# Half-size products from tile 4 on, tile 1 masked by VectorE, three general heads, a stepped write and engine orders from a table

## The chip, the cores and the metric

The kernel runs on one core of a Trainium2 chip. A core has five engines that run side by side and meet through semaphores: TensorE (PE, matrix products; PEld is its weight load), VectorE (DVE), ScalarE (ACT), GpSimd (POOL) and SyncE (SP, which here issues DMA). Matrix products go to an accumulator memory of eight banks per partition, which the program calls `banks`; ACT and DVE read them from there. The metric is the device time of one execution in microseconds (us).

## The reference

Causal attention with 4 batches, 8 heads, 768 positions and head size 64, and behind it a two-layer network over 3072 tokens:

```python
scores = scale * np.matmul(q, k.transpose(0, 1, 3, 2))
...
stream_keep = causal & (is_sink | in_win)
...
mask = np.where(retr[0, :, 0, 0, None, None], full_mask, stream_mask)
...
a = a / (np.sum(a, axis=-1, keepdims=True) + 1e-09)
return np.matmul(a, v).astype(np.float32)
```

```python
h = x @ w_in
g = h - np.tanh(h)
return (g @ w_out).astype(np.float32)
```

Retrieval heads (`is_retrieval`, three of eight here: heads 0, 2 and 6) see all earlier positions. The five other heads see only the first 4 positions (sinks) and a window of the last 64. `w_in` is 512 x 2048, `w_out` 2048 x 512.

## The kernel before

The 3072 tokens are cut into 12 tiles of 256 (`TT`), three per batch (`NG`); a tile is two blocks of 128. Heads go in pairs, `hp` 0 to 3, one head of a pair in partitions 0 to 63 and the other in 64 to 127.

**Attention of a tile.** q, k and v are loaded and turned to 16 bit. Up to tile 2, TensorE transposes q and k (`st_T`); from tile 3 on (`FROM`) a DMA does (`turn`). `st_S` (L1265) makes the scores of a pair, in groups of up to 512 columns per head, and ACT takes the exponential (L1362). `st_A` (L1421) multiplies with V; a column of ones gives the sum, DVE inverts it (L1462) and scales (L1474, L1489). Tiles 0 and 1 get their mask from TensorE, which adds it to the scores ahead of the products (`add`; `MASKS` is 2). Tile 0 uses per-head diagonals (`by_head`, L1308 and L1311), tile 1 the table `m4` (`masks`, L1074 and L1084, used in L1327). From tile 2 on DVE multiplies the exponentials with a mask (`mask`, L1371).

**Ranks.** `by_rank` (L1092) computes on the chip which heads are retrieval heads and sorts them to the front. From tile 3 on, GpSimd gathers q, k and v by rank (`gather`, L805). The first four ranks (`NGEN`) are general: they compute all earlier blocks, with a mask by flag. The last four are near heads: a query block takes its own block and the one before, and the sinks are packed into copies (`kc`, `vf`, by `gather` and `spread`). A pair is either general or near (`is_near`). A second program at the end repeats everything without ranks if more than `NGEN` heads are retrieval heads.

**The two layers.** `H_unit` (L1549) makes 2 x 128 columns of the first layer for 256 tokens, ACT the tanh (L1578) and DVE the difference (L1585) into `gt`. The second layer exists in two forms. `O_group` (L1614) has 16 products of 512 columns per block of 128 tokens, and ACT scales them out (L1598). From tile `ST` = 7 on, a scheme for 2 x 2 blocks takes seven products in place of eight: each has half the depth and half the columns, 8 matmuls of 256 columns (`piece`, L1725). For it DVE adds and subtracts parts of `gt` in fp16 (`sums`, L1700) and, once, parts of `w_out` (`combine`, L1660). The products come together again by ACT (`take`, L1783), DVE (`fold`, L1802) and POOL (`add`, L1813); `STEPS` says in which of the eight units of the next tile. In every third such tile (`mixed`), the tokens of a pair of rows are dealt out to the two halves, so the first layer reads x with a step of two.

**Order.** The program is not written in engine order. Each operation is given to `Plan` (L145) with an engine, an estimated duration and what it reads and writes. `Plan.run` simulates the engines when the kernel is built, picks on each the waiting operation with the lowest priority number, and emits the instructions in that order. The number is the place in the program plus an entry of the table `NUDGE`. Constants such as `CUT`, `LEAD`, `LD`, `GA` and `TWHEN` say beside which unit the attention, the loads, the gathers and the combinations are put. Each engine then runs its instructions strictly in the emitted order. DMAs are issued from SP, POOL and ACT.

Of the kernel before, what the change touches and what calls it, by code (L numbers as in the profile page):

```python
# [12 lines left out]
TT = 256  # L13
# [3 lines left out]
NUDGE = {  # L17
# [127 lines left out]
class Plan:  # L145
# [11 lines left out]
    GRAB = 350  # L157
    RESULT = {"PE": 200, "ACT": 0, "DVE": 0, "POOL": 0, "SP": 0}

    def __init__(self, bufs, nudge):  # L160
        self.bufs, self.nudge = bufs, nudge
        self.users = {}
        self.ops = []
# [223 lines left out]
def kernel(  # L387
# [109 lines left out]
    ST = 7  # L497
# [1755 lines left out]
```

## Time and profile before

| what | value |
|---|---|
| median of 3 runs | 226.71 us (226.59 to 226.87) |
| the profiled execution | 228.01 us |
| its span, first to last instruction | 226.2 us |
| mean granted TensorE clock | 1.000 |
| moved by DMA | 35.33 MB, 156 GB/s |
| TensorE's last product ends | about 222.2 us |

In the page, a row of an instruction group gives the line, engine, operation, output and inputs by the program's names, shape and count; then the busy time in us, the mean of one in ns, and the idle time ahead of them with the releaser. A matmul lies in a pipeline, so its own duration (273 ns for 256 columns) is longer than its pace. The chain that ended last is followed back from the last instruction, at each step to what released it.

### The profile page before, as it was taken

The page shows a single profiled execution, that of the slowest core. Times are in us where ns is not written, and L with a number is a line of the kernel's source. Part 1 is how long each engine was busy: PE and PEld are TensorE (multiplying, and loading weights), DVE is VectorE, ACT ScalarE, POOL GpSimd, SP SyncE. Part 2 cuts the span into 40 slices and gives each one's busy share as a digit, 9 for nine tenths or more (in the row PEclk, how much of TensorE's full clock was granted, in tenths as well). Part 3 has the DMA queues.
Part 4 walks back from the last instruction along what each step waited for, and adds up shares of the span by engine and source line. Part 5 has one row for each costly group of instructions (what it writes and reads, how often), then busy time and mean ns, then how long its engine had stood idle before and what let it go on. Part 6 is the DMA issues. An engine that isn't in the chain of part 4 may idle for free.

```text
span 226.2 us, 6489 instructions
## 1 busy us (share of the span) xinstructions
PE 216.8 (96%) x2442; PEld 168.4 (74%) x2442; DVE 172.5 (76%) x443; ACT 143.8 (64%) x225; POOL 111.9 (49%) x243
## 2 busy tenths in 40 slices
PE   7799899999799999999999999999999999999992
PEld 6467687878686766767757777676898888988881
DVE  6887897594975965768997754879989789368973
ACT  5878769875467868755675786486667667246410
POOL 8999262696937468438823936971004031021121
PEclk9999999999999999999999999999999999999999
DMA  6999999998999999999979999944301701302022
GB/s 179 171 191 205 194 200 227 242 196 199 244 192 243 181 210 171 248 187 213 253 145 241 206 244 168 210 116 93 96 3 48 92 5 51 91 3 93 0 96 101
DMA packets 104133, 35.33 MB, mean 156 GB/s; under 512 B 90658, under 2 KB 102434, under 8 KB 104098
## 3 DMA queue, kind: packets, MB, share of 16 engines
q1 hardware_dynamic: 86128, 26.75, 59.9%
q0 software_dynamic: 17152, 7.60, 25.5%
q10 hardware_dynamic: 818, 0.52, 0.8%
q8 instruction: 20, 0.33, 0.6%
q14 instruction: 15, 0.12, 0.2%
HBM read 27.26 MB, written 6.29 MB: 148 GB/s over the span
## 4 chain that ended last, share of the span: by engine, by line
PE 82%; DVE 12%; ACT 2%; DMA 1%; issue 1%; DVEq 0%; POOL 0%; POOLq 0%; ACTq 0%
PE banks L1566 34%; PE banks L1624 21%; PE banks L1748 11%; PE banks L1349 7%; PE banks L1442 7%; DVE gt L1585 2%; PE banks L2085 1%; DVE pt L1413 1%; ACT th L1578 1%; DVE x L1489 1%; DMA out_dram<-ot 1%; DVE t L1209 1%; DVE m L1715 1%; DVE t L1062 1%; DVE ot L1802 1%
## 5 line engine op out<-in xcount | busy, mean ns | idle before, releaser
L1566 PE MATMUL banks<-xT,win 128*128 128x256 f16 x768 | 95.5, 273 | 0.4 <-DVE gt L1585 0.2
L1566 PEld LDWEIGHTS <-win 128*128 128x128 f16 x768 | 72.6, 98 | 13.9 <-issue 1.3
L1578 ACT ACTIVATE th<-banks 128x512 f32<-128x512 f32 x96 | 56.5, 600 | 34.4 <-PE banks L1566 30.4
L1585 DVE SCALAR_TENSOR_TENSOR gt<-th,banks 128x512 f16<-128x512 f32 x88 | 59.1, 681 | 17.1 <-ACT th L1578 16.8
L1362 ACT ACTIVATE pt<-banks 128x768 f16<-128x768 f32 (+1 forms) x60 | 53.1, 919 | 14.0 <-PE banks L1349 13.8
L1624 PE MATMUL banks<-wout,gt 128*128 128x256 f16 (+1 forms) x256 | 48.4, 326 | 0.0
L817 POOL CAST t<-rawqk 128x256 f16 x72 | 27.3, 420 | 13.7 <-DMA rawqk<-in_k_dram 8.4
L1813 POOL TENSOR_TENSOR ot<-gu,ot 128x256 f32<-128x256 f32 x8 | 6.5, 818 | 52.4 <-ACT gu L1783 43.3
L1624 PEld LDWEIGHTS <-gt 128*128 128x128 f16 x256 | 23.5, 98 | 11.5 <-issue 0.8
L853 POOL CAST v<-rawv 128x128 f16 x72 | 23.8, 369 | 9.4 <-DMA rawv<-in_v_dram 9.4
L1474 DVE TENSOR_TENSOR x16t<-banks,rinv 128x128 f32 (+1 forms) x80 | 22.3, 287 | 1.2
L1349 PE MATMUL banks<-QK 64*128 64x128 f16 (+1 forms) x364 | 21.0, 238 | 0.5 <-ACT QK L1207 0.5
L1413 DVE TENSOR_TENSOR pt<-pt,m4r 128x1024 f16<-128x1024 f16 (+1 forms) x18 | 15.3, 852 | 6.4 <-ACT pt L1362 6.2
L1362 ACT ACTIVATE ptn<-banks 128x1024 f16<-128x1024 f32 (+1 forms) x18 | 17.1, 951 | 4.7 <-PE banks L1349 4.7
L1442 PEld LDWEIGHTS <-pt 128*128 128x128 f16 x420 | 15.9, 97 | 4.8 <-issue 1.6
L1349 PEld LDWEIGHTS <-QK 64*128 64x128 f16 x364 | 12.6, 94 | 8.8 <-issue 6.8
L1442 PE MATMUL banks<-v,pt 128*128 128x65 f16 x220 | 16.4, 193 | 1.6 <-DVE pt L1413 1.2
L1748 PEld LDWEIGHTS <-m 128*128 128x128 f16 x160 | 15.2, 98 | 2.3 <-issue 0.5
L1462 DVE RECIPROCAL rinv<-banks 128x4 f32<-128x4 f32 x48 | 8.5, 178 | 10.7 <-PE banks L1442 9.7
L1384 DVE TENSOR_TENSOR ptn<-ptn,mS 128x1024 f16<-128x1024 f16 x12 | 8.5, 705 | 6.6 <-ACT ptn L1362 6.4
L842 POOL COPY kc<-QK 128x128 f16<-128x128 f16 x12 | 5.0, 417 | 16.8 <-DMA QK<-t 16.8
L1442 PE MATMUL banks<-vf,pt 128*128 128x65 f16 x200 | 13.2, 193 | 0.0
(120 smaller groups left out, 270.3 us busy)
## 6 DMA issues: line engine op xcount, KB each, us to landing
rawqk<-in_q_dram SPq DMA_DIRECT2D x18, 256.0 KB, 4.4
out_dram<-ot SPq DMA_DIRECT2D x18, 256.0 KB, 2.4
rawqk<-in_k_dram SPq DMA_DIRECT2D x17, 256.0 KB, 4.4
rawv<-in_v_dram SPq DMA_DIRECT2D x16, 256.0 KB, 4.7
win<-in_moe_w_in_dram POOLq DMA_DIRECT2D x4, 512.0 KB, 10.5
wout<-in_moe_w_out_dram POOLq DMA_DIRECT2D x4, 512.0 KB, 12.9
out_dram<-ot SPq DMA_DIRECT2D x10, 128.0 KB, 3.2
v<-in_v_dram POOLq DMA_DIRECT2D x6, 128.0 KB, 8.3
```

The costliest lines, as they stand in the source:

```text
L817: nc.gpsimd.tensor_copy(out=c5()[:, :, :, s_ : s_ + 1, :], in_=r5()[:, :, :, at, :])
L853: nc.gpsimd.tensor_copy(out=v1s[b]()[:, g * NB : g * NB + NB, RANK[s_] : RANK[s_] + 1, 0:D], in_=rv()[:, :, at, :],)
L1349: nc.tensor.matmul(out=sc()[:, hh, o : o + nb * 128], lhsT=lhsT, rhs=QK[p_, hp, q_0 : q_0 + nb * 128], start=not added, stop=not added or ...
L1362: lambda pt=pt, sc=sc, gi=gi, wid=wid: nc.scalar.activation(out=pt()[:, :, 512 * gi : 512 * gi + wid], in_=sc()[:, :, 0:wid], func=AF.Exp, ...
L1413: nc.vector.tensor_mul(out=pv, in0=pv, in1=m)
L1442: nc.tensor.matmul(out=av()[:, i, hh, :], lhsT=pt()[:, hh, co : co + 128], rhs=vv, start=(jb == first_jb), stop=(jb == qb),)
L1474: nc.vector.tensor_mul(out=xt()[:, :, at, :], in0=av()[:, :, hh : hh + 1, 0:D], in1=rinv()[:, :, hh : hh + 1].unsqueeze(3).to_broadcast([1 ...
L1566: nc.tensor.matmul(out=ph()[:, j, :], lhsT=w_in_t[fb // 4][:, cb, f0 : f0 + 128], rhs=x, start=(cb == 0), stop=(cb == HP - 1),)
L1578: lambda: nc.scalar.activation(out=th()[:], in_=ph()[:], func=AF.Tanh, scale=1.0 / XS),
L1585: lambda: nc.vector.scalar_tensor_tensor(out=gt()[:, u * FU : (u + 1) * FU, :], in0=th()[:], scalar=-XS, in1=ph()[:], op0=ALU.mult, op1=AL ...
L1624: nc.tensor.matmul(out=po()[:, c0:c1], lhsT=gt()[:, f, ts * 128 : ts * 128 + 128], rhs=w_out_t[:, f, c0:c1], start=(f == 0), stop=(f == NF ...
L1748: nc.tensor.matmul(out=po()[:, at : at + CM], lhsT=lhs(c), rhs=rhs(c), start=c == 0, stop=c == NC - 1,)
```

## The change

The table `NUDGE` goes. In its place stands `TURN`, a list of operation numbers, and `Plan` lets an engine take only the operation whose turn it is:

```diff
-        prio = (i if prio is None else prio) + self.nudge.get(i, 0)
+        prio = i if prio is None else prio
...
+        lists = {e: iter([i for i in self.turn if self.ops[i][0] == e]) for e in self.ENGINES}
+        turns = {e: next(lists[e], None) for e in self.ENGINES}
...
+            if self.turn and turns[self.ops[i][0]] != i:
+                return 1e12
...
-                top = self.APART[0] if self.ops[i][5] >= self.split else self.FIXED
+                top = self.APART[0] if self.turn or self.ops[i][5] >= self.split else self.FIXED
...
+            if self.turn and i is not None:
+                return [(a, (b,)) for b, a in one.items()]
```

Constants: general heads, the first tile of the seven-product form, copies by engine, and places in the program.

```diff
-    NGEN = H // 2
+    NGEN = 3
...
-    TE = (('DA', 'DA', 'DD', 'DD'), ('DD', 'DD', 'DA', 'DD'), ('AA', 'AD', 'AA', 'DD'))
-    XE = ('DADA', 'ADAD')
+    TE = (('DA', 'DD', 'DA', 'DD'), ('DA', 'AD', 'AA', 'DD'), ('AA', 'AD', 'AA', 'DD'))
+    XE = ('AADA', 'DAAA')
...
-    CUT1 = (-9.0, -5.0, 2.25, 13.0)
+    CUT1 = (-12.0, -3.0, -0.75, 13.5)
...
-    ST = 7
+    ST = 4
...
-    TG = 5
+    TG = 2
...
-    TWHEN = ((4, 0), (8, 0), (8, 1))
+    TWHEN = ((2, 1), (4, 7), (5, 1))
...
-    LEAD = 4
-    FIN = 0
+    LEAD = 3
+    FIN = 1
...
-    QUART = 7
-    LD = 14
-    GA = 11
+    QUART = 4
+    LD = 19
+    GA = 14
...
-    BR = 1
+    BR = 8
...
-    NE = "DDDDDDDD"
-    MS = 1
+    NE = 'DAADDDAA'
+    MS = 0
...
-    IE = ("ACT", "DVE")
+    IE = ('DVE', 'ACT')
...
-    MK = "DDAADDAD"
+    MK = 'PDPDDPDP'
...
-    MASKS = 2
...
-    A2 = (3, 6)
+    A2 = (3.0, 9)
```

Inside the program `MASKS` is 1 (0 in the second program), so TensorE adds the mask of tile 0 alone. `m4` now holds ones and zeros, of which the first program makes only columns 256 to 511, on DVE and POOL; the ACT form, `thr2` and `minus` go. Tiles 1 and 2 are masked by one DVE multiplication per pair (`tensor_mul`) in place of two `scalar_tensor_tensor`.

With three general ranks, pair 2 is split: one head general, one near (`is_half`). Its first score group holds the general head's columns beside the near head's; the rest goes to the general head alone, in one group over both banks.

```diff
+        def is_half(n):
+            return ranked(n // HP) and n % HP == 2
...
+            if is_half(n) and g == 2:
+                return [GROUPS[2][0], GROUPS[2][2] + GROUPS[2][1]]
...
+                            out=(
+                                flat[:, o : o + nb * 128] if solo
+                                else sc()[:, hh, o : o + nb * 128]
+                            ),
...
+            near = [is_near(n) or (is_half(n) and hh == 1) for hh in range(2)]
...
+            low = [max(qb - 1, 0) if x else 0 for x in near]
```

The copies `kc` and `vf` cover the pairs and heads that this makes near. The mixed tiles read x straight and deal out the tokens where they write:

```diff
-                        x = xT()[:, :, cb, :]
+                        h_, x = ph()[:, j, :], xT()[:, :, cb, :]
                         if mixed(t):
-                            x = x.rearrange("p i (a two) -> p two i a", two=2)
+                            h_ = h_.rearrange("p (two i a) -> p i a two", two=2, i=NB)
+                            x = x.rearrange("p i (a two) -> p i a two", two=2)
                         nc.tensor.matmul(
-                            out=ph()[:, j, :], lhsT=w_in_t[fb // 4][:, cb, f0 : f0 + 128],
+                            out=h_, lhsT=w_in_t[fb // 4][:, cb, f0 : f0 + 128],
```

Beside these, many estimated durations of `Plan` are set anew, the model's stall of DVE behind POOL is widened, and the last tile's products come in the order of `finale` in place of `finale_b`.

More of the change, by code (lines that the diff above doesn't have):

```diff
@@ L353, in run @@
             queue[e].remove(i)
+            turns[e] = next(lists[e], None)
             _, ns, _, _, dma, _, port = self.ops[i]
@@ L368, in run @@
                 held = (t + self.GRAB if dma else t, free[e])
-            elif port and held[0] <= t < held[1]:
-                ns += held[1] - t
-                free[e] += held[1] - t
+            elif port and t < held[1] and t + ns > held[0]:
+                stall = held[1] - max(t, held[0])
+                ns += stall
+                free[e] += stall
             if dma:
@@ L451 @@
     rflag0 = const.tile([128, H], FP32, name="rflag0")
-    thr2 = const.tile([128, H], FP32, name="thr2")
-    minus = const.tile([128, 128], FP16, name="minus")
     coef = const.tile([128, H], FP32, name="coef")
-    m4r = const.tile([128, NGEN, 512], FP16, name="m4r")
+    m4r = const.tile([128, NGEN + 1, 512], FP16, name="m4r")
     rflagr = const.tile([128, NGEN], FP32, name="rflagr")
@@ L458 @@
     thrr = const.tile([128, NGEN], FP32, name="thrr")
-    mS = const.tile([128, 5, 128], FP16, name="mS")
+    mS = m4r[:, NGEN, :]
     iota = const.tile([128, H], FP32, name="iota")
@@ L531 @@
     RL = (1100, 1500)
-    A2 = (3, 6)
+    A2 = (3.0, 9)
     ORDER = ('t1', 0, 'v1', 1, 2, 3, 4, 5, 't2', 'r3', 6, 7)
     def program(first):
-        P = Plan(bufs, NUDGE if first else {})
+        P = Plan(bufs, TURN if first and fast else ())
         op = P.op
@@ L588, in ranked @@
             return first and fast and t >= NG
+        MASKS = 1 if first else 0
         QKs, v1s, vfs, kcs, t16s, raws, packed = {}, {}, {}, {}, {}, {}, {}
@@ L840, in gather @@
                 op(
-                    "POOL", 340,
+                    "POOL", 400,
                     lambda jb=jb: nc.gpsimd.tensor_copy(
@@ L845, in gather @@
                     ),
-                    r=[qk_keys(b, g, jb % NB, 1, hp) for hp in (1, 3)], w=[("kc", b, jb)],
+                    r=[qk_keys(b, g, jb % NB, 1, hp) for hp in range(1, HP)], w=[("kc", b, jb)],
                     prio=len(P.ops) + 8,
@@ L859, in gather @@
                     "POOL", 325, vv, r=["regsPOOL"] + [("rawv", iv, i) for i in range(NB)],
-                    w=[("v1", b, g * NB + i, RANK[s_] // NGEN) for i in range(NB)],
+                    w=[("v1", b, g * NB + i, int(RANK[s_] >= NGEN)) for i in range(NB)],
                 )
@@ L879, in spread @@
                 op(
-                    "POOL", 1060,
+                    "POOL", 1300,
                     lambda: nc.gpsimd.tensor_copy(
@@ L1015, in flags @@
                 ),
-                r=["rflag"], w=["coef"],
+                r=["rflag"], w=["coef"], port=True,
             )
@@ L1022, in flags @@
                 ),
-                r=["rflag"], w=["thr"],
-            )
-            op(
-                "ACT", 200,
-                lambda: nc.scalar.activation(
-                    out=thr2[:], in_=rflag[:], func=AF.Copy, scale=-0.5, bias=1.0
-                ),
-                r=["rflag", "warm"], w=["thr2"],
-            )
-            op(
-                "DVE", 110,
-                lambda: nc.vector.tensor_scalar(
-                    out=minus[:], in0=ident16[:], scalar1=-60000.0, scalar2=None, op0=ALU.mult
-                ),
-                r=["ident"], w=["minus"], port=True,
+                r=["rflag"], w=["thr"], port=True,
             )
@@ L1060, in by_head @@
                 op(
-                    "DVE", 130,
+                    "DVE", 190,
                     lambda h=h: nc.vector.tensor_scalar(
@@ L1234, in st_T @@
                 op(
-                    e, {"ACT": 400, "DVE": 430}[e],
+                    e, {"ACT": 450, "DVE": 435}[e],
                     lambda x=x, e=e: copy(
@@ L1251, in program, with is_near, near_pieces, near_reads @@
         }
-        COL = {g: {} for g in range(NG)}
-        for g in range(NG):
-            for gi, grp in enumerate(GROUPS[g]):
+        pts = {}
+        def is_near(n):
+            return ranked(n // HP) and n % 2
+        def is_half(n):
+            return ranked(n // HP) and n % HP == 2
+        def near_pieces(g):
+            out = []
+            for i in range(NB):
+                qb = g * NB + i
+                for jb in (qb, qb - 1) if g else range(qb + 1):
+                    out.append((jb, i, 1, 128 * len(out), 0 < jb < qb))
+            return out
+        def near_reads(b, hp, pieces):
+            r = []
+            for jb, i, nb, o, comp in pieces:
+                r += (
+                    [("kc", b, "low"), ("kc", b, jb)] if comp
+                    else [qk_keys(b, jb // NB, jb % NB, 1, hp)]
+                )
+            return r
+        def far_groups(n):
+            g = n // HP % NG
+            if is_near(n):
+                return [None]
+            if is_half(n) and g == 2:
+                return [GROUPS[2][0], GROUPS[2][2] + GROUPS[2][1]]
+            return GROUPS[g]
+        def columns_of(n):
+            at = {}
+            for gi, grp in enumerate(far_groups(n)):
                 o = 512 * gi
@@ L1274, in st_S @@
                 sc, key = bank([128, 2, 512], FP32, "sc", f"sc{n}_{gi}")
-                pieces = []
+                half = is_half(n)
                 if near:
-                    o = 0
-                    for i in range(NB):
-                        qb = g * NB + i
-                        for jb in (qb - 1, qb):
-                            if jb >= 0:
-                                pieces.append((jb, i, 1, o, 0 < jb < qb))
-                                reads += (
-                                    [("kc", b, "low"), ("kc", b, jb)] if 0 < jb < qb
-                                    else [qk_keys(b, jb // NB, jb % NB, 1, hp)]
-                                )
-                                o += 128
-                else:
-                    o = 0
-                    for jb, q0, nb in GROUPS[g][gi]:
-                        pieces.append((jb, q0, nb, o, False))
+                    pieces = [(hh, *x) for x in near_pieces(g) for hh in range(2)]
+                    reads += near_reads(b, hp, near_pieces(g))
+                    o = 128 * len(near_pieces(g))
+                else:
+                    o, own = 0, []
+                    for jb, q0, nb in far_groups(n)[gi]:
+                        own.append((jb, q0, nb, o, False))
                         reads.append(qk_keys(b, jb // NB, jb % NB, 1, hp))
                         o += 128 * nb
+                    if not half:
+                        pieces = [(hh, *x) for x in own for hh in range(2)]
+                    elif gi:
+                        pieces = [(0, *x) for x in own]
+                    else:
+                        beside = near_pieces(g)
+                        reads += near_reads(b, hp, beside)
+                        pieces = sorted(
+                            [(0, *x) for x in own] + [(1, *x) for x in beside],
+                            key=lambda x: (x[4], x[0]),
+                        )
                 reads += [qk_keys(b, g, i, 0, hp) for i in range(NB)]
@@ L1296, in st_S @@
                 ns += o * 0.44
-                if gi == 0 and first and t in TW:
+                if gi == 0 and t < MASKS:
                     def add(n=n, g=g, hp=hp, sc=sc, wid=o):
@@ L1319, in st_S @@
                         w=[key] + ["add"] * (t == 0))
-                elif gi == 0 and t < MASKS:
-                    def add(n=n, g=g, hp=hp, sc=sc, wid=o):
-                        for hh in range(2):
-                            m = m4[:, 2 * hp + hh, 0:384]
-                            if g:
-                                m = m4[:, 2 * hp + hh, 256:512].unsqueeze(1).to_broadcast([128, 2, 256])
-                            nc.tensor.matmul(
-                                out=sc()[:, hh, 0:wid],
-                                lhsT=(minus if MK[2 * hp + hh] == "A" else ident16)[:], rhs=m,
-                                start=True, stop=False,
-                            )
-                    op("PE", 2 * o * 0.427 + 60, add, r=[("m4", hp), "ident", "minus"] + ["visit"] * (t > 0),
-                        w=[key] + ["add"] * (t == 0))
@@ L1335, in st_S @@
-                todo.append((n, gi, b, g, hp, near, sc, key, pieces, o))
+                todo.append((n, gi, b, g, hp, near, half and gi, sc, key, pieces, o))
             def mm():
-                for n, gi, b, g, hp, near, sc, key, pieces, wid in todo:
+                for n, gi, b, g, hp, near, solo, sc, key, pieces, wid in todo:
                     QK = QKs[b]()
                     added = gi == 0 and n // HP < MASKS
-                    for jb, q0, nb, o, comp in pieces:
-                        for hh in range(2):
-                            p_ = slice(64 * hh, 64 * hh + 64)
-                            kk = QK[p_, HP + hp, :]
-                            lhsT = kk[:, jb * 128 : jb * 128 + 128]
-                            if comp:
-                                lhsT = kcs[b]()[p_, hp // 2, jb - 1, :]
-                            q_0 = g * TT + q0 * 128
-                            nc.tensor.matmul(
-                                out=sc()[:, hh, o : o + nb * 128], lhsT=lhsT,
-                                rhs=QK[p_, hp, q_0 : q_0 + nb * 128], start=not added,
-                                stop=not added or o + nb * 128 == wid,
-                            )
+                    flat = sc()[:].rearrange("p a c -> p (a c)")
+                    for hh, jb, q0, nb, o, comp in pieces:
+                        p_ = slice(64 * hh, 64 * hh + 64)
+                        kk = QK[p_, HP + hp, :]
+                        lhsT = kk[:, jb * 128 : jb * 128 + 128]
+                        if comp:
+                            lhsT = kcs[b]()[p_, hp - 1, jb - 1, :]
+                        q_0 = g * TT + q0 * 128
+                        nc.tensor.matmul(
+                            out=(
+                                flat[:, o : o + nb * 128] if solo
+                                else sc()[:, hh, o : o + nb * 128]
+                            ),
+                            lhsT=lhsT, rhs=QK[p_, hp, q_0 : q_0 + nb * 128], start=not added,
+                            stop=not added or o + nb * 128 == wid,
+                        )
@@ L1355, in st_S @@
             op("PE", ns, mm, r=reads, w=keys + ["visit"])
-            for n, gi, b, g, hp, near, sc, key, pieces, wid in todo:
+            for n, gi, b, g, hp, near, solo, sc, key, pieces, wid in todo:
                 pt, ip = pts[n]
@@ L1662, in combine @@
             op(
-                "DVE", 90 + 860 * 2 // TQ,
+                "DVE", 320,
                 lambda: getattr(nc.vector, fn)(
@@ L1952, in batch_visits @@
                 units += [(a, i) for i in range(g + 1)] + [(d, 0)]
-                units += [(c, i) for i in range(g + 1)] + [(e, 0)]
+                units += [(c, i) for i in range(len(far_groups(c)))] + [(e, 0)]
             return [units[i : i + 3] for i in range(0, len(units), 3)]
@@ L2120, in program @@
             spread_over(qs[: 4 * TQ], slot_of[TWHEN[0]], slot_of[TWHEN[1]])
-            assert TWHEN[2][0] == ST + 1
+            at = [slot_of[x] for x in TWHEN]
+            assert TWHEN[2][0] == ST + 1 and 3 * at[1] + at[0] >= 4 * slot_of[4, 0]
             spread_over(qs[4 * TQ :], slot_of[TWHEN[2]], slot_of[TWHEN[2]])
@@ L2204, in program @@
             (finale if FIN else finale_b)(last)
-            leave_behind(last, "E", 0)
+            leave_behind(last, "F", 0)
         else:
```

168 lines of the change are left out of this document (68 added, 100 removed), and 196 rows, old and new, of tables (NUDGE, TURN).

## The prediction

> **What bounds the kernel now.** I read the page's busy times first, then the chain that ended last, then the windows by stage.
>
> ```profile
> span 226.2 us, 6489 instructions
> PE 216.8 (96%) x2442; PEld 168.4 (74%) x2442; DVE 172.5 (76%) x443; ACT 143.8 (64%) x225; POOL 111.9 (49%) x243
> PE 82%; DVE 12%; ACT 2%; DMA 1%; issue 1%; DVEq 0%; POOL 0%; POOLq 0%; ACTq 0%
> ```
>
> TensorE is busy for 96% of the span and carries 82% of the chain. The windows (time, then PE, PEld, DVE, ACT, POOL busy) show where that holds:
>
> ```profile
> 0.00:60.00 60.00, 54.71 (x699) 43.15 (x700) 46.97 (x139) 44.67 (x74) 43.85 (x80) 1.00 1.30 202
> 60.00:150.00 90.00, 90.00 (x972) 63.93 (x969) 65.71 (x165) 60.91 (x90) 55.45 (x146) 1.00 1.11 206
> 150.00:190.00 40.00, 40.00 (x466) 32.94 (x464) 35.46 (x92) 25.91 (x40) 6.75 (x12) 1.00 0.27 54
> 190.00:213.00 23.00, 23.00 (x234) 20.71 (x233) 16.63 (x34) 10.62 (x19) 2.87 (x4) 1.00 0.19 58
> 213.00:227.00 14.00, 9.06 (x82) 7.71 (x79) 7.71 (x17) 1.72 (x4) 2.97 (x4) 0.96 0.23 80
> ```
>
> From 60 to 213 us PE has no gap; at a granted clock of 1.00 a matmul removed there shortens the span by its own pace. Before 60 us PE lacks 5.29 of 60 us and the chain hops between DVE, ACT and PE, so a removal counts only in part. Busy time overlaps in the pipeline, so I take the pace of a matmul from the chain of waits, where pieces follow one another (start, length, what):
>
> ```profile
> 16.33 0.43 PE banks L1327 x2
> 63.54 5.24 PE banks L1566 x48
> 95.35 0.78 PE banks L1442 x26
> 106.20 1.73 PE banks L1624 x8
> 123.38 0.72 PE banks L1349 x18
> 172.47 2.72 PE banks L1566 x24
> 210.11 3.49 PE banks L1748 x32
> ```
>
> Pace is length over count: 216 ns for a 512-wide output product (L1624), 109 ns for a 256-wide one (L1748), 215 ns for a mask product of 512 columns (L1327), 30 ns for a 65-wide product with V (L1442), 109 ns for a 256-wide product of the first layer (L1566), and 113 ns for that product in tile 9 (the row at 172.47, in the tenth group of 64), which reads every second token.
>
> **The change part by part, as PE time.**
>
> *Half-size products from tile 4 on (ST 7 to 4).* Tiles 4, 5 and 6 each trade 2 x 16 products of 512 columns, 32 x 216 = 6.91 us, for 7 x 8 of 256 columns, 56 x 109 = 6.10 us. Three times 0.81 is **-2.43 us**, all in the stage without PE gaps. The weight loads rise from 32 to 56 per tile; at 98 ns (rows below) they fit under 109 ns, as they already do in L1748.
>
> The Trainium skill, "TensorE: Matmul & The Clock Gate", section "Back-to-back issue gap", gives a sustained 131 ns for a 512-column matmul in a stream with its weight load. By it the old form would cost 4.2 us per tile and the new one more. The trace contradicts it: eight such pairs took 1.73 us, so nothing here rests on it.
>
> *Tile 1 masked by VectorE (MASKS 2 to 1).* Eight L1327 products leave PE: 8 x 215 = 1.72 us. They stood at 12 to 23 us, where PE has gaps; with nothing of it realised it is 0, with all of it -1.72, and I take **-1.1**, nearer to the whole, since PE is still busy for over nine tenths of that stage. DVE gets four masks in their place (0.78 us each, L1413 below), behind each exponential; PE's products with V for that head pair wait for them. The twelve-odd small instructions that rank the heads (by_rank) move later (BR 1 to 8) and make the room on DVE.
>
> *Three general heads (NGEN 4 to 3).* In each batch of tiles 3 to 11 one head goes from all earlier blocks to two per query block: 3+4 becomes 4 and 5+6 becomes 4, so 3 + 7 products with V fall away per batch, 30 in all, 30 x 30 ns = **-0.90 us**. Score products save nothing on PE: the 18 products at 123.38 are 1536 columns per head, 0.65 us at L1566's pace, and both heads together took 0.72, so the heads run side by side and the partner still pays its own columns. Taking half away leaves the length; I take 0, with 0.3 us of loss if products without a partner run less densely, and no gain. ACT's exponentials shrink by 384 + 896 columns per batch, which no wait of PE in that stage asks for.
>
> *The step of two on the written accumulators.* Tile 9's 64 products read at 113 ns; reading straight at 109 saves 64 x 4 = **-0.27 us**. Tiles 6 and 9 then write with a jump between neighbouring columns, which no row shows. From below it costs nothing (109 ns); from above, if each written column took twice its time, 128 x 109 = 13.95 us. The nearest row is the stepped read, 4 ns dearer than a plain one, so I take no extra.
>
> The Trainium skill, "PSUM — Partial Sum Buffer", section "Specifications (TRN2)", says that any non-contiguous access pattern slows matmuls significantly, because of 8-byte lines there. No run so far shows it for a matmul's write; it is the page behind the third rival.
>
> *The start.* Here ACT is in the way (engine, line and operation; the bracket is idle time and its releaser):
>
> ```profile
> 4.70 1.95 ACT L1074 ACTIVATE m<-A,thr 128x512 f16<-128x512 f16 x3
> 6.55 1.12 ACT L1207 CAST t<-rawqk 128x512 f16<-128x512 f32 x2
> 7.21 0.62 PE L1226 MATMUL banks<-ident,t 128*128 128x128 f16 x8 [0.87 <-ACT t L1207]
> ```
>
> The loads behind those casts, by the timeline and by the list of DMA issues (KB each, median us to landing):
>
> ```profile
> 1.43 1.05 SPq L622 DMA_DIRECT2D rawqk<-in_q_dram  x2
> ...
> rawqk<-in_q_dram SPq DMA_DIRECT2D x18, 256.0 KB, 4.4
> ```
>
> PE's first transposes wait for a cast that waits on ACT behind three masks (1.95 us). They move to DVE and POOL, at half the width. Half of the by_head instructions come to ACT instead; at 0.21 us each on DVE (rows below, 1.7 us for 8) up to twice that on ACT, two ahead of the cast are 0.4 to 0.8. The first casts can come up to 1.5 us sooner, the second half only as its load lands: issued by 2.5, with 4.4 us as the median to landing, so at about 6.9, against a present cast start of about 7.1. Between 0 and 1.5 I take **-0.7**.
>
> *VectorE and GpSimd.* The rows for DVE's new work:
>
> ```profile
> L1715 DVE TENSOR_TENSOR m<-gt 128x512 f16<-128x512 f16 x20 | 9.3, 472 | 0.0
> L1715 DVE TENSOR_TENSOR m<-m,gt 128x512 f16<-128x512 f16 x10 | 4.1, 422 | 0.1
> L1715 DVE TENSOR_TENSOR m<-gt,m 128x512 f16<-128x512 f16 x10 | 4.1, 420 | 0.1
> L1802 DVE SCALAR_TENSOR_TENSOR ot<-banks,gu 128x512 f32<-128x512 f32 x4 | 2.7, 687 | 0.5 <-PE banks L1748 0.4
> L1413 DVE TENSOR_TENSOR pt<-pt,m4r 128x1024 f16<-128x1024 f16 x12 | 9.4, 782 | 2.7 <-ACT pt L1362 2.7
> L1403 DVE SCALAR_TENSOR_TENSOR pt<-m,pt 128x512 f16<-128x512 f16 x8 | 6.0, 788 | 0.8 <-ACT pt L1362 0.8
> L1062 DVE TENSOR_SCALAR t<-ident,coef 128x128 f16<-128x128 f16 x8 | 1.7, 383 | 0.0
> L1748 PEld LDWEIGHTS <-m 128*128 128x128 f16 x160 | 15.2, 98 | 2.3 <-issue 0.5
> ```
>
> Sums cost (9.3 + 4.1 + 4.1) / 5 = 3.5 us per tile, two folds 1.4: three tiles, +14.7. Tile 1's masks are +3.1. Tile 2's masks become the packed form, 4 x 0.78 for 6.0, -2.9; by_head -0.8; moved copies and smaller masks about -3. DVE ends near 183.5 of 222 us, 83%. In the stage from 60 to 150 it is 65.71 + 14.7 = 80.4 of about 87 us, 92%. The cover is PE's own work: between 150 and 190 DVE ran at 35.46 of 40 (89%) and PE never waited. At 92% I allow **+0.6** for waits; without cover see the second rival. POOL gains three additions per tile, nine of about 0.8 us, and stays below 60%; the chain never rests on it.
>
> *The table of orders.* It replaces the planner's priorities. As before, the program for each engine is fixed when it is built, so no wait is added as such; what it shifts can be seen in no row. I bound it by the 5.29 us that PE lacks before 60 us (gain) and by what DVE can cost (loss, below), and take 0. The other ending (FIN 1) also stays at 0: the timeline's last products stand 0.30 us behind the ones before, and the fold and store behind them remain.
>
> ```profile
> 221.16 1.03 PE L1748 MATMUL banks<-wout,m 128*128 128x256 f16 x8
> 221.16 0.75 PEld L1748 LDWEIGHTS <-m 128*128 128x128 f16 x7 [0.30 <-issue]
> ```
>
> **The sum.** -2.43 - 1.1 - 0.90 - 0.27 - 0.7 + 0.6 = -4.8 us. The profiled execution took 228.01 us, its span 226.2 with 1.81 around it; the median of the runs is 226.71, 1.30 less. The differences apply to either, so 228.01 becomes 223.2, and the median becomes **221.9 us**.
>
> **The rivals.**
>
> *1. The new order also closes PE's early gaps.* For it: one gap has a clear cause, a DVE mask held for 2.98 us beside a POOL cast group, with PE waiting 1.25 behind it:
>
> ```profile
> 55.65 2.80 POOL L817 CAST t<-rawqk 128x256 f16 x8
> 55.88 2.98 DVE L1413 TENSOR_TENSOR pt<-pt,m4r 128x768 f16<-128x768 f16 x1 [1.94 <-ACT pt L1362]
> 58.92 0.35 PE L1442 MATMUL banks<-v,pt 128*128 128x65 f16 x6 [1.25 <-DVE pt L1413]
> ```
>
> Against it speaks the row of the slices: DMA is nearly full from the start, and the weights' landing sets when work can begin.
>
> ```profile
> DMA  6999999998999999999979999944301701302022
> ```
>  Half of the 5.29 us and the rest of the mask products: -3.2, so 218.7.
>
> *2. VectorE takes PE's place between 60 and 150 us (the slower side).* The sums now run while POOL reads SBUF (55.45 of 90 us busy there, 6.75 of 40 where they run today). The view of L1715 gives their spread:
>
> ```profile
> L1715 DVE TENSOR_TENSOR m<-gt x20: 410/419/953, 145.8 to 218.1; 128x512 f16<-128x512 f16 x20
> ```
>
> The longest took 953 ns against a median of 419, 0.53 more. If each of the 24 new ones were held so, 12.8 us join 80.4: 93.2 of DVE work in a stage that PE needs 87 us for, +6 us: 228. It is slower than before once the hold passes (90 - 80.4) / 24 = 0.40 us on each. A partial form, a third of it and some waits around, gives back half of the gain: 224.5. The Trainium skill, "SBUF — State Buffer", section "Who interferes with whom", has the same mechanism: a DVE instruction with two SBUF inputs contends with a GpSimd instruction that reads SBUF. The 2.98 us mask above agrees.
>
> *3. The stepped write doubles the products of tiles 6 and 9.* +13.95 on the sum: 235.9. It turns the result slower from 38 ns per product (4.8 us / 128). Against it speaks only the mild cost of the stepped read.
>
> *4. The program does more than it says:* with three general heads, the second program runs if more than three heads are retrieval heads; the reference sets exactly three, so no.
>
> **How the numbers follow.** A difference within 0.2% (0.45 us) cannot be told from no change. My forecast, 220.3 to 223.3, gets 0.48; rival 1 0.17; rival 2 in part (224 to 226.5) 0.17, in full 0.08; rival 3 0.08; the rest 0.02. Faster holds the first two and most of the partial form, 0.81; same 0.04; slower 0.15. The range, 218.4 to 226.5, reaches from rival 1 to the partial rival 2 and leaves out rival 3 and the full rival 2.
>
> **What would show it.** Right: output products of 256 columns at 109 ns from tile 4 on, about 3 us less in the stage from 60 to 213, no L1327, first transposes before 6.8 us, DVE near 183 us. Wrong: first-layer products of tiles 6 and 9 above 113 ns; sums near 0.9 us and PE idle behind DVE between 90 and 150; PE lacking more than 5.3 us before 60.

## The result, and the profile after

| | time | to before |
|---|---|---|
| before | 226.65 us (226.42 to 226.87) | 1 |
| after | 239.54 us (237.4 to 240.8) | 1.0559 [1.0482, 1.0636] |
| forecast | 221.9 us (218.4 to 226.5) | 0.979 |

The kernel became 12.9 us slower. The forecast said 4.8 faster, and the time lies 13.0 us above the range. The times in this document are medians over the executions that did not fall into a slower state with a lower granted clock. The changed kernel's page, its span, busy times and the engines' shares of the chain:

```profile
span 235.6 us, 6542 instructions
PE 225.8 (96%) x2457; PEld 180.3 (77%) x2457; DVE 185.1 (79%) x460; ACT 138.7 (59%) x227; POOL 125.5 (53%) x256
PE 72%; DMA 12%; POOL 7%; DVE 5%; issue 2%; ACT 0%; DVEq 0%; POOLq 0%
```

PE's share of the span is what it was, 96%, so nothing here says which work became dearer. DMA and POOL now carry 19% of the chain; they carried 1% before. The same windows as before (time, then PE, PEld, DVE, ACT, POOL busy, clock, DMA share, GB/s):

```profile
0.00:60.00 60.00, 55.85 (x716) 45.20 (x717) 42.98 (x127) 45.02 (x79) 41.51 (x69) 1.00 1.25 189
60.00:150.00 90.00, 88.35 (x922) 66.92 (x921) 74.18 (x186) 54.40 (x84) 56.82 (x137) 1.00 1.08 201
150.00:190.00 40.00, 40.00 (x382) 32.19 (x381) 33.56 (x74) 19.74 (x33) 18.85 (x38) 1.00 0.33 74
```

From 150 to 190 us PE is busy throughout, as before, but handles 382 products in place of 466. The chain of waits gives the pace (start, length, what):

```profile
94.09 11.35 PE banks L1510 x104
...
128.49 6.04 PE banks L1510 x28
135.24 7.01 PE banks L1510 x32
...
175.70 3.45 PE banks L1510 x16
179.33 3.46 PE banks L1510 x16
...
220.64 10.93 PE banks L1692 x100
```

The first layer's products (L1510) run at 11.35 / 104 = 109 ns in tiles 4 and 5. In tile 6 (from 128 us) and tile 9 (from 176) they take 7.01 / 32 = 219 and 3.45 / 16 = 216 ns. These are the two tiles with the stepped write. The output products (L1692) have 256 columns at 109 ns, as forecast. 128 products by 107 ns are 13.7 us: that is the third rival, named in the prediction at a chance of 0.08.

### The profile page after: what moved, and what is told of

The parts are those of the page before. It is cut to its first block, busy times and chain, and to the rows that moved or that the text cites. A ratio compares the mean times of both kernels' runs of the same rounds, so it can differ in the third digit from the quotient of the medians.

```text
span 235.6 us, 6542 instructions
## 1 busy us (share of the span) xinstructions
PE 225.8 (96%) x2457; PEld 180.3 (77%) x2457; DVE 185.1 (79%) x460; ACT 138.7 (59%) x227; POOL 125.5 (53%) x256
## 4 chain that ended last, share of the span: by engine, by line
PE 72%; DMA 12%; POOL 7%; DVE 5%; issue 2%; ACT 0%; DVEq 0%; POOLq 0%
PE banks L1510 35%; PE banks L1692 19%; PE banks L1568 9%; DMA t16p<-in_k_dram 5%; PE banks L1381 5%; PE banks L1293 5%; DMA wout<-in_moe_w_out_dram 4%; DMA t16p<-in_q_dram 2%; POOL v L615 1%; POOL rawqk L726 1%; DVE ot L1746 1%; DVE m L1659 1%; POOL vf L861 1%; POOL t16p L649 1%; POOL m L1015 1%
## 5 line engine op out<-in xcount | busy, mean ns | idle before, releaser
L1510 PE MATMUL banks<-xT,win 128*128 128x256 f16 x768 | 105.9, 297 | 0.7 <-DMA win<-in_moe_w_in_dram 0.7
L1510 PEld LDWEIGHTS <-win 128*128 128x128 f16 x768 | 77.8, 104 | 18.6 <-DMA win<-in_moe_w_in_dram 1.1
L1314 ACT ACTIVATE pt<-banks 128x1024 f16<-128x1024 f32 (+3 forms) x57 | 49.0, 907 | 4.6 <-PE banks L1293 4.3
L771 POOL CAST t<-rawqk 128x256 f16 x72 | 30.3, 457 | 18.3 <-DMA rawqk<-in_q_dram 13.7
L1692 PEld LDWEIGHTS <-m 128*128 128x128 f16 x256 | 24.3, 98 | 4.9 <-issue 1.3
L1568 PE MATMUL banks<-wout,gt 128*128 128x256 f16 (+1 forms) x160 | 26.0, 295 | 0.7 <-DMA wout<-in_moe_w_out_dram 0.7
L1692 PEld LDWEIGHTS <-gt 128*128 128x128 f16 x192 | 18.3, 98 | 2.7 <-issue 0.3
L1757 POOL TENSOR_TENSOR gu<-gu 128x256 f32<-128x256 f32 x7 | 5.3, 758 | 26.5 <-ACT gu L1727 26.5
L1568 PEld LDWEIGHTS <-gt 128*128 128x128 f16 x160 | 13.7, 98 | 5.5 <-issue 1.8
L1692 PE MATMUL banks<-wout,m 128*128 128x256 f16 x128 | 16.9, 273 | 0.9 <-DVE x16t L1417 0.8
L1692 PE MATMUL banks<-wout,gt 128*128 128x256 f16 x128 | 17.5, 273 | 0.0
L1659 DVE TENSOR_TENSOR m<-gt 128x512 f16<-128x512 f16 x32 | 16.7, 531 | 0.1
```

The source lines that it names most:

```text
L771: nc.gpsimd.tensor_copy(out=c5()[:, :, :, s_ : s_ + 1, :], in_=r5()[:, :, :, at, :])
L1314: nc.scalar.activation(out=o_, in_=i_, func=AF.Exp, scale=inv_sqrt_d)
L1510: nc.tensor.matmul(out=h_, lhsT=w_in_t[fb // 4][:, cb, f0 : f0 + 128], rhs=x, start=(cb == 0), stop=(cb == HP - 1),)
L1568: nc.tensor.matmul(out=po()[:, c0:c1], lhsT=gt()[:, f, ts * 128 : ts * 128 + 128], rhs=w_out_t[:, f, c0:c1], start=(f == 0), stop=(f == NF ...
L1659: lambda k=k, fn=fn, a=a, b=b, cs=cs: getattr(nc.vector, fn)(out=S4[k][:, cs, :], in0=a()[:, cs, :], in1=b()[:, cs, :]),
L1692: nc.tensor.matmul(out=po()[:, at : at + CM], lhsT=lhs(c), rhs=rhs(c), start=c == 0, stop=c == NC - 1,)
```

## The experiments: the write

Two theories stood after the result. A: the stepped write doubles 128 products, and this is the whole loss. B: something else in the change (orders, VectorE) costs a good part of it. Every kernel below ran beside runs of the kernel before on the same chip (226.5 us each time), and the ratios are to those.

**The changed kernel again,** unchanged.

> The changed kernel unaltered, for its spread on this chip and as the partner of the next three. Both theories: 237 to 241 us, first-layer products of tiles 6 and 9 at 216 ns each and all others at 109 ns.

238.5 us (238.07 to 239.59), 1.0542 [1.0511, 1.0572]. The loss repeats.

**The changed kernel with the stepped read of before.**

```diff
                         if mixed(t):
-                            h_ = h_.rearrange("p (two i a) -> p i a two", two=2, i=NB)
-                            x = x.rearrange("p i (a two) -> p i a two", two=2)
+                            x = x.rearrange("p i (a two) -> p two i a", two=2)
```

> The changed kernel with one part undone: tiles 6 and 9 read x with a step of two and write straight, as before. Theory A (the stepped write alone makes the change slow): 114 ns per product in tiles 6 and 9, 128 x 102 = 13.1 us off, so 226.4 us from the median of 239.5, and 224.3 from the profiled execution of 237.4. Theory B (the new order and the load on VectorE make it slow, the stepped write only fills idle time): TensorE waits elsewhere instead, less than 5 us off, above 234 us. If all other terms of the prediction held, 221.9 plus 0.6.

225.53 us (225.41 to 225.71), 0.9958 [0.9943, 0.9972]: 13.0 us less than the changed kernel. Its chain, in tiles 4 and 5, 6 and 9:

```profile
93.68 11.35 PE banks L1509 x104
...
132.27 3.73 PE banks L1509 x32
...
172.23 1.81 PE banks L1509 x16
```

That is 109 ns, 117 (the median of tile 6 is 113) and 113. A stands, B falls for the loss.

**The kernel before with the stepped write,** which there touches tile 9 alone (the same two lines the other way round).

> The kernel before with the stepped write in place of the stepped read; only tile 9 is dealt out there. Theory A: 216 ns in place of 114 in 64 products, +6.5 us, 233.2 us. Theory B: the write costs nothing by itself where the order is tuned, 226 to 228 us.

233.17 us (233.08 to 234.53), 1.0312 [1.028, 1.0345]. 64 x (216 - 113) ns = 6.6 us on 226.5 are 233.1. Nothing hides the products: PE has no gaps there.

**Pairs of neighbours.** Tokens are dealt out two at a time, so that each write fills two neighbouring columns (8 bytes) before it jumps. The rows then lie in pairs, and each store of these tiles becomes two DMAs. The main lines of the edit:

```diff
-                            h_ = h_.rearrange("p (two i a) -> p i a two", two=2, i=NB)
-                            x = x.rearrange("p i (a two) -> p i a two", two=2)
+                            h_ = h_.rearrange("p (two k q) -> p k two q", two=2, q=2)
+                            x = x.rearrange("p i (k two q) -> p i k two q", two=2, q=2)
```

> The changed kernel, with tokens of tiles 6 and 9 dealt out in pairs: two neighbouring columns are written next to each other, then the jump; the stores of these tiles go in two DMAs each, four more in all. Theory A with lines of 8 bytes: 109 ns per product, 13.7 us off, 225.8 us from the median. Theory A where any jump halves the pace: 216 ns, 239 us. Theory B: above 234 us.

226.29 us (225.33 to 227.62), 0.9981 [0.9942, 1.0019]. The spread is too wide to tell the pairs from the stepped read (225.53) in time; the pace tells. The chain in tile 9 has a plain one, 1.75 / 16 = 109 ns:

```profile
174.09 1.75 PE banks L1510 x16
```

**A survey of patterns,** one per tile, in a single run.

> One pattern of writing per tile of the first layer; the tokens of tiles 4, 5, 7, 8, 10 and 11 come out in another order (and some columns of tile 10 not at all), so only the pace of a product is read. Tile 4: neighbouring pairs, each pair far from the next; tile 5: fours, far jumps; tiles 6 and 9: single columns, far jumps, as in the changed kernel; tile 7: every second column, then the others; tile 11: single columns that jump by two inside groups of four; tile 8: straight write, stepped read; tile 10: pairs that begin on an odd column (252 columns, 48 of the 64 products). Theory of 8-byte lines: 109 ns in tiles 4 and 5, 216 in 6, 7, 9 and 11, 113 in 8; tile 10 at about 212, since no pair fills a line. Rival, any jump costs: 216 in tiles 4 and 5 too. Rival, only a far jump costs: 109 in tiles 7 and 11, 216 in 4, 5, 6 and 9. Rival within the lines, two neighbours suffice wherever they begin: tile 10 at 107 to 109. Whole time by the first theory: 225.5 of the kernel that reads with a step, plus 4 x 64 x 0.107 = 27.4, plus 48 x 0.104 = 5.0: about 258.

255.55 us, 2.4 less than that sum; where the 2.4 went was not followed up. The chain of waits, first-layer products only:

```profile
93.74 11.35 PE banks L1525 x104
...
134.18 7.01 PE banks L1525 x32
...
148.84 4.32 PE banks L1525 x20
...
173.81 2.72 PE banks L1525 x24
...
185.38 3.45 PE banks L1525 x16
...
210.72 0.75 PE banks L1525 x4
...
224.22 8.63 PE banks L1525 x40
```

From the top: tiles 4 and 5 (pairs, fours, far jumps) 109 ns; tile 6 (singles, far jumps) 219 and tile 9, the fifth row, 216; tile 7 (every second column) 216; tile 8 (stepped read) 113; tile 11 (singles that jump by two within four) 216. The distance of the jump doesn't matter, whether two neighbours follow one another does. Tile 10 mixes one plain product of 256 columns with three of 252 in pairs from an odd column: (750 - 109) / 3 = 214 ns. So a pair must also begin on an even column: a line of 8 bytes explains every row, and neither "any jump" nor "far jumps" does. A plain write that begins on an odd column was not run.

The Trainium skill has this in two forms. "PSUM — Partial Sum Buffer", "Specifications (TRN2)", says any non-contiguous pattern slows matmuls; tiles 4 and 5 contradict that. "Advanced Engine Details and Errata", "PSUM Cachelines", adds that every two consecutive elements should be contiguous; the rows agree for pairs from an even column, not for those from an odd one, and put the price at about twice (216 ns for 109).

## The experiments: where the other gains went

With the read in place the kernel is 1.0 us faster. The other terms of the prediction, without the 0.27 for the read, gave 4.5. A profile of an ordinary execution of the kernel before was taken to compare with.

> The kernel before, unchanged, for a profile of an ordinary execution beside the experiments: 226.5, span 224.8.

226.5, span 224.8. I worked PE's idle time out of the traces: the time from one matmul's start to the next, less the pace of its shape in an unbroken stream (109 ns for 256 columns, 216 for 512, 29 for 65). The last two columns are of versions with two and four entries of the table moved, which follow below.

```
us of the span      before  stepped read  2 moved  4 moved
  0 to  20            5.9       7.1         6.9      7.1
 20 to  60            3.8       3.2         3.3      4.6
 60 to 110            2.1       1.8         2.3      1.9
110 to 130            0.6       3.5         3.5      2.1
130 to 170            1.3       1.3         1.3      1.3
170 to 190            0.7       2.2         1.0      1.0
190 to the end        0.3       0.2         0.3      0.1
all idle             14.7      19.4        18.6     18.1
all work            204.6     198.9       198.9    198.9
```

Work fell by 5.7 us. The forecast's removals are 2.43 + 1.72 + 0.90 = 5.05; ten fewer warm-up products of 56 ns are the rest. So the terms of work were right. 4.7 us came back as idle time: 0.6 before 60 us, 2.9 from 110 to 130 and 1.5 from 170 to 190.

**Without the table:** `Plan` gets an empty list and orders by its own priorities.

```diff
-        P = Plan(bufs, TURN if first and fast else ())
+        P = Plan(bufs, ())
```

> The kernel that reads with a step (225.53), without the table: the planner's own priorities set every engine's order. Theory that the table costs nothing and gains nothing, as forecast: 225.0 to 226.0. Theory that the table is what closes the gaps from 20 to 60 us: slower by the 2.2 us that were won there or more, above 227.5. Theory that the table's order causes the waits from 110 to 130 and 170 to 190 us: faster, 221 to 224.

227.09 us (226.83 to 227.54), 1.0023 [1.0013, 1.0033]: 1.6 slower. The table costs nothing on the whole. Without it PE waits elsewhere: 2.7 us from 20 to 30, where the kernel with the table has 0.9.

**The kernel before without its nudges** (`Plan(bufs, {})`).

> The kernel before without its table of nudges: the planner's priorities set the orders, as in the other kernel without a table (227.09). If the parts of the change are worth the 4 to 5 us of the forecast wherever the orders come from: 231 to 232. If the load on VectorE eats what TensorE saves, with any order: 226.5 to 228.5. In between, the difference to 227.09 is what the parts are worth without tables.

228.66 us (228.56 to 229.03), 1.0099 [1.0082, 1.0117]. The old table had been worth 2.1 us, the new one is worth 1.6. Without either, the parts of the change gain 228.66 - 227.09 = 1.6 us, not 4 to 5, and not even that lies on PE. The last products of the kernel before, with its nudges:

```profile
219.75 1.03 PE L1748 MATMUL banks<-wout,m 128*128 128x256 f16 x8
```

and without:

```profile
219.65 1.04 PE L1748 MATMUL banks<-wout,m 128*128 128x256 f16 x8
```

PE ends at 220.8 us with the nudges and at 220.7 without. Their 2.1 us lie behind it: the last store is issued at 221.3 and 221.4 us and lands at 223.0 and 225.0, for a reason that no run shows. The new table is worth 1.1 us on PE itself, which ends at 219.7 us with it and at 220.8 without. Without tables the change took 5.4 us of work off PE and gave it 5.6 us of idle time, so the larger part of the shortfall is no matter of one table.

**Smaller sums.** The sums of tiles 5 and 6 leave out three quarters of their columns here, and only the time is read.

```diff
-                    cs = slice(h * NC // SH, (h + 1) * NC // SH)
+                    cs = slice(h * NC // SH, h * NC // SH + (1 if t in (5, 6) else NC // SH))
```

> The kernel that reads with a step (225.53), with the same orders, but VectorE's sums of tiles 5 and 6 work on a quarter of their columns (three quarters are left out): 16 sums become some 0.3 us shorter, 5 us less VectorE work between 100 and 150 us. Theory that VectorE's load makes PE wait there: the idle time of PE from 110 to 130 us falls from 3.5 to below 1.5, and the time by 1.5 to 3, to 222.5 to 224.0. Rival, that PE waits there for the order of the table or for GpSimd and not for load: within 0.5 of 225.5.

225.6 us (225.02 to 225.75): no faster. PE's idle time from 110 to 130 fell to 2.2, but 0.9 more before 60 us and 0.5 more from 60 to 110, stages that the edit hardly touches, took that back in the profiled execution. The timeline of the kernel with the stepped read shows why the size helped little (start, length, engine, line):

```profile
118.63 1.46 POOL L835 COPY vf<-v 64x1300 f16<-64x1300 f16 x1
118.88 1.48 DVE L1658 TENSOR_TENSOR m<-gt,m 128x512 f16<-128x512 f16 x1
...
121.81 1.03 PE L1691 MATMUL banks<-wout,m 128*128 128x256 f16 x8 [0.99 <-DVE x16t L1417]
```

and with a quarter of the columns:

```profile
119.66 1.26 POOL L835 COPY vf<-v 64x1300 f16<-64x1300 f16 x1
...
119.72 1.29 DVE L1658 TENSOR_TENSOR m<-gt,m 128x128 f16<-128x128 f16 x1
```

A sum of 0.41 us took 1.48 beside a POOL copy, and a quarter of it still took 1.29: DVE isn't slowed in proportion; both sums end 0.1 to 0.3 us behind the copy, as if DVE stood until it was done. The Trainium skill, "SBUF — State Buffer", "Who interferes with whom", names the pair: a DVE instruction with two inputs in SBUF contends with one of GpSimd that reads SBUF. The trace agrees.

**That copy given to VectorE** (`"DVE" if b else "POOL"`, from the second batch on).

> The kernel that reads with a step (225.53), with GpSimd's copy of V for the sinks (64x1300, 1.46 us beside a sum that took 1.48) given to VectorE from the third tile on, same orders. Theory that a GpSimd instruction holds a VectorE sum for its whole length: the sum at about 119 us falls from 1.48 to 0.41, VectorE pays the copy itself (an estimate from its 128x512 f16 copy of 0.29: 0.75), PE's idle time from 110 to 130 us falls from 3.5 to 2.5 to 3.2, time 224.6 to 225.3. Rival, that the sum was long for another reason: the sum stays, VectorE only gets 0.75 more, 225.7 to 226.5.

226.12 us (224.71 to 227.21), 0.9976 [0.9957, 0.9994], which settles nothing in time. In the trace the sum took 0.73 us, the copy 0.48 on DVE, and PE's idle time from 110 to 130 fell to 2.6, but in the profiled execution the last store ended 1.1 us later, though PE's last product ended 0.5 us sooner.

**Two entries of the table moved:** the scalings 1046 and 1045 (V for tile 9) go ahead of addition 1336, for PE waited there for POOL:

```profile
171.89 0.19 PE L1381 MATMUL banks<-vf,pt 128*128 128x65 f16 x1 [1.04 <-POOL vf L826]
```

> The kernel that reads with a step (225.53), with two entries of the table moved: GpSimd scales V for tile 9 (two instructions, L826) ahead of three additions for an output tile, not behind them. Theory that the 1.0 us wait of PE at 172 us is GpSimd's queue, whose head waits 1.6 us for a fold of VectorE: the wait goes, PE's idle time from 170 to 190 us falls from 2.2 to about 1.0, time 224.3 to 224.9. Rival, that VectorE is as late there and the next wait takes its place: 225.3 to 225.7.

224.16 us (223.82 to 224.78), 0.989 [0.9876, 0.9904]; 1.4 faster than with the stepped read alone, a little more than expected. Two windows of the kernel with the stepped read alone:

```profile
110.00:130.00 20.00, 18.13 (x244) 15.03 (x243) 19.50 (x47) 13.08 (x18) 13.20 (x26) 1.00 1.12 205
...
170.00:190.00 20.00, 18.96 (x244) 16.12 (x242) 17.86 (x41) 11.61 (x18) 5.11 (x10) 1.00 0.41 102
```

and the second of them with the entries moved:

```profile
170.00:190.00 20.00, 20.00 (x255) 17.19 (x253) 18.47 (x45) 12.48 (x19) 4.15 (x8) 1.00 0.41 106
```

PE lacks nothing there now (the first window shows DVE at 19.50 of 20 us, of which more below). POOL's queue runs in order: an addition at its head waited 1.6 us for a late fold of DVE, and scalings that needed nothing stood behind it. This version is faster than both kernels, by 1.1% against the one before.

**Both edits together.**

> Both of these edits in one kernel. If the two waits are separate: the sum of the two gains, 223.5 to 224.6. If PE only waits elsewhere: 225.2 to 225.7.

225.24 us (224.66 to 225.8), 0.9943 [0.9929, 0.9957]. They don't add up. In its trace PE waits 1.04 us for the output weights at 49.9 us.

**The copy moved, not given away:** entries 686 and 754 (the copy and a scaling) go ahead of cast 838, into a gap of POOL while DVE reads PSUM; the two entries above stay moved.

> The kernel with two entries of the table moved (224.16), and two more of GpSimd's entries moved: the copy of V for the sinks (L831, 64x1300) and one scaling of V (L822) run in the 4.4 us in which GpSimd sits idle from 104 us, while VectorE reads PSUM, and not at 118.6 us beside the sums. Nothing is left out or given to another engine. Theory that the hold was what made VectorE late there: the sum of 1.48 us falls to 0.41 and its neighbours too, PE's idle time from 110 to 130 us falls from 3.5 to 1.0 to 2.0, time 222.6 to 223.4. Rival, that VectorE is full there anyway (19.50 of 20 us busy) and PE waits for its load: the sum falls, but the idle time stays above 2.5 and the time at 223.7 to 224.4.

224.22 us (223.47 to 224.43), 0.9886 [0.9868, 0.9904]. Its timeline:

```profile
50.67 0.38 PE L1563 MATMUL banks<-wout,gt 128*128 128x256 f16 x2 [1.77 <-DMA wout<-in_moe_w_out_dram]
...
120.19 0.41 DVE L1654 TENSOR_TENSOR m<-gt,m 128x512 f16<-128x512 f16 x1
```

The copy runs at 105.2 us, the sum is back at 0.41, and the idle time from 110 to 130 fell from 3.5 to 2.1: half of the excess went with the copy and the scaling. For the other half DVE's load is the likeliest cause, since the smaller sums, with the copy in its place, took 1.3 us off too. Two waits of PE for DVE are left in this trace, 0.36 us for a sum and 0.48 for a fold. The time stayed: in the profiled execution the wait for output weights took 1.77 us.

**The wait for the output weights.** Neither profile of before has it. The last load of these weights was issued there at 33.4 us (its timeline):

```profile
33.41 0.88 POOL L795 DMA_DIRECT2D wout<-in_moe_w_out_dram  x1 [0.22 <-issue]
```

After the change, here with the stepped read, POOL first waits:

```profile
33.02 0.91 POOL L726 DMA_DIRECT2D rawqk<-in_k_dram  x1 [6.29 <-DVE gt L1528]
...
38.50 1.77 POOL L749 DMA_DIRECT2D wout<-in_moe_w_out_dram  x2
```

By the program, what POOL waits for is the load of the ranks of the heads into its registers, and BR 8 has moved the ranking on DVE behind other work. In the last experiments the two loads go ahead of that register load. The second of them also writes in pairs.

```diff
+            for i in (81, 82):
+                order.remove(i)
+                order.insert(order.index(314), i)
```

> The kernel with four of GpSimd's entries moved (224.22; 222.5 span, 1.8 us of PE's wait at 50 us in it), and the last two loads of the output weights issued ahead of the register load for which GpSimd waits 6.3 us from 26.4 us on, so at about 27 and not at 38.5 and 39.4 us; the issue orders of the other engines stay. Theory that everything TensorE gains in the first 49 us is taken back by the landing of these weights (49.2 us, 33.4 us was their last issue in the kernel before): they land by about 42, the wait of PE on that load goes, PE's idle time from 0 to 60 us falls by 0.3 to 1.8, time 222.6 to 223.7. Rival, that the DMA queues are full for the first 50 us and the loads that now come later (Q, K and V of the next batch) make the next wait: 224.0 to 225.5.

> The same kernel, with tiles 6 and 9 written in neighbouring pairs with a straight read (109 ns in place of 113) and their stores in two DMAs each. If only the products count: 128 x 4 ns, 0.5 us faster than the other. If the further stores cost as much as they save: the same within 0.3.

228.92 us (1.0111 [1.0092, 1.0131]) and 228.09 (1.0068 [1.0055, 1.0081]). Both are slower than anything expected. The rival had the mechanism, but its range ended at 225.5: the wait on the weights went, and a longer one came. From the first one's timeline:

```profile
36.19 0.90 POOL L615 DMA_DIRECT2D v<-in_v_dram  x1
...
45.86 0.21 PE L1381 MATMUL banks<-v,pt 128*128 128x65 f16 x1 [4.14 <-DMA v<-in_v_dram]
```

V of the next batch landed 9.6 us after its issue. The wait is 2.4 us longer than the one for the weights had been. The rest of the loss is the clock: behind the wait it was 0.50, and eight products of 256 columns took 1.90 us in place of 1.04. From 45.9 to 51.3 us PE ran so, which cost about 2.7 us. A window of that stretch (the clock is the third figure from the end):

```profile
46.00:51.00 5.00, 5.00 (x54) 3.74 (x53) 1.09 (x5) 1.33 (x3) 5.00 (x19) 0.50 0.38 84
```

In both orders of loads one was late in the first 50 us; that every order must have a late one was not shown. The pairs were 0.8 us faster, which the spread of the runs (228.25 to 229.93 against 227.89 to 228.83) doesn't tell from the 0.5 of their products.

## Why the prediction was wrong

**The step that failed** is "The step of two on the written accumulators": "The nearest row is the stepped read, 4 ns dearer than a plain one, so I take no extra." The write took 107 ns more per product, not 0. The upper bound, 13.95 us, was right to 0.3. The rival's "from 38 ns per product" was too high, since it rested on a gain of 4.8 us: the change without the write gained 1.0, and 1.5 with both tiles read straight, by 128 x 4 ns, so about 12 ns per product would have used it up. The row I called nearest measures another memory and another direction: x is read from SBUF, the product is written to PSUM. No row of before bore on the write, so the chance of 0.08 had no ground in the profile. With 107 ns in that step the sum gives 235.6, and 3 to 4 us are still missing.

**The removals on PE** were right: 96 products of 512 columns became 168 of 256, eight mask products and 30 products with V went, at the paces of the rows; 5.05 us forecast, 5.7 measured with the warm-up products.

**The start, -0.7, and the masks of tile 1, -1.1,** were right as a sum, with luck in the parts. Of the masks' 1.72 us I let 0.6 turn into idle time and took 0.7 of other idle time away, so -0.1 in all; measured is +0.6 up to 60 us, of which the missing warm-up products are 0.56. The first transposes came sooner, as forecast (6.13 us with the stepped read, 7.49 in the second profile of before). Yet PE's idle time rose by 1.2 in the first 20 us and fell by 0.6 from 20 to 60, for which I had no term. The first rival, which closes half of the early gaps, did not come.

**VectorE, +0.6,** is the second step that failed: behind 60 us PE's idle time rose by 4.0. The load was right (185.1 us after, 183.5 forecast). The cover was not: "between 150 and 190 DVE ran at 35.46 of 40 (89%) and PE never waited" was carried over to a stage where it ran at 19.50 of 20. There PE's idle time rose by 2.9 us, of which the trace with the stepped read gives 1.75 to three waits for DVE (0.99, 0.27 and 0.49); a late fold cost another 1.2 through POOL's queue at 172. This is the second rival in its partial form. Its mechanism is clearest in one sum (the view of L1658 with the stepped read):

```profile
L1658 DVE TENSOR_TENSOR m<-gt,m x16: 409/418/1480, 107.3 to 216.1; 128x512 f16<-128x512 f16 x16
```

The longest took 1.07 us too much, twice the 0.53 of before; but the median stayed. The 26 sums that start between 60 and 150 us took 3.6 us longer than at 0.415 each, 0.14 on average, so the 0.53 that the rival put on each was far too high. With the copy and one scaling moved it was 1.3 us.

**The table, 0:** it is worth 1.6 us against no table, the one that it replaced 2.1, all of it behind the last product. So the exchange lost about 0.6 us, and in the new table sat a fault of 1.4 us that two entries mend.

Left open: 1.5 us of idle time from 110 to 130 us, of which 0.84 are waits for DVE in the trace, without a run that removes both causes at once; why the last store of the kernel without nudges lands 2 us late; and what the first 60 us could give with a better order of loads.

## What to carry to other kernels

Where a change makes TensorE write its accumulators in another order, look at the smallest run of neighbouring columns: two fp32 values that begin on an even column are free, single ones cost twice, whatever the jump. A bound that nothing in the trace narrows is a case of its own with a real chance, and the nearest row counts only if it measures the same memory in the same direction. Where the work taken off the bounding engine raises the load of one that was at nine tenths, read each in-order queue behind that engine: a head that waits there delays work that needs nothing from it.

## What the runs showed of the hardware

- A write of single columns with a jump between them doubles a 256-column product (216 ns for 109), pairs from an odd column nearly so (214 ns for 252 columns); a read of every second fp16 column costs 4 ns.
- A VectorE sum took 1.48 us at 512 columns beside a GpSimd copy of 1.46 us, and 1.29 at 128 columns beside one of 1.26.
- Where PE waited 4.14 us, in the kernel with the two loads moved, the granted clock fell to 0.50 (46 to 51 us, the window above) and stood at 1.00 again from 51.3 us; with the pairs on top, the wait was 4.2 us and the clock did the same. In the profiles of the other orders it is 1.00 until PE's work ends, beside waits of up to 1.8 us.
